# A one-column exponential behind each Gelu pass of a fused attention and MLP kernel

## The chip, the cores and the metric

The kernel runs on one core of one Trainium2 chip. The metric is the device time of one execution in microseconds; lower is better. The engines are called by short names in the profile: PE is TensorE (matmuls; PEld its weight loads), DVE is VectorE, ACT is ScalarE, POOL is GpSimd, SP is SyncE, which issues most of the DMAs.

## The reference

For one sequence of 2048 tokens of width 512 it computes two branches from the same input and mixes them by a gate of each token:

```python
g = _sigmoid((x * gate_w).sum(-1, keepdims=True))
a = _A_ref(x, A_wqkv, A_wo)              # attention, 32 heads of 16
b = _B_ref(x, B_w1, B_w2, B_w3, B_w4)
return g * a + (1 - g) * b

def _B_ref(x, w1, w2, w3, w4):
    h = _gelu(_layernorm(x, axis=-1) @ w1)
    ...   # four quarters of h shifted by 1, -1, 2, -2 tokens
    x1 = x + hs                          # hs: the shifted quarters @ w2
    h2 = _gelu(_layernorm(x1, axis=-1) @ w3) @ w4      # w3: 512 x 1792
    return x1 + h2
```

The Gelu is the tanh form. The attention is a full softmax: 32 heads times 2048 x 2048 scores.

## The kernel before, in words

The attention sets the length. Its scores are made in blocks of 128 keys by 512 queries. TensorE writes such blocks into the eight banks of PSUM (the product of q and kT, line 1320). Most blocks go to ScalarE, two at a time: one instruction takes the exponential of 128x1024 scores from the banks and writes it as bf16 into `prob` (line 1415). The other blocks go to VectorE, which makes an approximate exponential by working on the bits (line 1446) and adds shifts of it (line 1489); GpSimd makes a part of these shifts (line 1491). TensorE then multiplies the blocks of `prob` with V (line 1544). A slot of `prob` may be written again when the product that read it is done.

Between the attention's matmuls stand those of the MLP branch (helper `gen`, line 953): `w1`, then the first Gelu, then `w2`; later `w3`, the second Gelu, and `w4`. `hT` holds the first hidden layer, 128 x 4 x 2048. The second hidden layer, of width 1792, is worked on in chunks of 512 tokens, two chunks at a time (`PAIRS`), one in `hB` and one in the memory of `hT`. A Gelu is one ScalarE instruction over a whole layer or chunk, in place. So ScalarE makes three Gelu passes: one instruction of 128x8192 (`mlp1`, line 1187), and twice two instructions of 128x7168 (`mlp2`, line 1224). Everything else that ScalarE does is exponentials, besides a few copies at both ends.

The exponential and the Gelu need different function tables in ScalarE. The compiler puts a table load ahead of each activation whose function isn't in the table that is loaded: seven loads in all, one at the start, one ahead of each Gelu pass, and one ahead of the first exponential behind each pass. The program books a load to the line of the activation it belongs to. If an activation waits for several semaphores, the waits that don't fit on it stand ahead of it in the queue of its engine, and ahead of its table load.

The order of the instructions on each engine is set before the program runs. `Sim` is a model of the engines with costs written down in the kernel; `act(hold, deps, fn)` gives it a ScalarE job with an assumed duration and a function that emits the instruction. `Sim` plays the jobs through and writes down the order, and the functions are called in that order. The chip then runs each engine's instructions in that fixed order and holds an instruction back only until the data and buffers it needs are there. Small constant tiles that the change touches: `zero` (128x384, zeros, bf16) and `mb` (128x1, 32-bit), which at the start of the program helps to make the masks `mO` and `mE` and is not read later. At the start there is already one exponential of a column of `zero` (line 928), which brings the first table load.

Of the kernel before, what the change touches and what calls it, by code (L numbers as in the profile page):

```python
# [10 lines left out]
ACT = mybir.ActivationFunctionType  # L11
ALU = mybir.AluOpType
BF16 = mybir.dt.bfloat16
F32 = mybir.dt.float32
# [438 lines left out]
def kernel(  # L453
# [14 lines left out]
    nc = tc.nc  # L468
# [3 lines left out]
    S, D = x_flat.shape  # L472
    H, DH = 32, 16
    KT = D // P
# [3 lines left out]
    FT = F // P  # L478
# [268 lines left out]
    zero = const.tile([P, 384], BF16, name="zero")  # L747
# [8 lines left out]
    mb = const.tile([P, 1], mybir.dt.int32, name="mb")  # L756
# [8 lines left out]
    hT = const.tile([P, KT, S + 4], BF16, name="hT")  # L765
# [58 lines left out]
    def act(hold, deps, fn, **kw):  # L824
        return sim.add(Job("ACT", hold, 180.0, deps, fn, **kw))

    def gp(hold, deps, fn, **kw):
        return sim.add(Job("POOL", hold, 110.0, deps, fn, port=True, **kw))
# [15 lines left out]
    def W(name):  # L844
        return wb[name].slot
# [11 lines left out]
    def start(eng, lat, fn, hold=530.0):  # L857
# [11 lines left out]
                                                   in_=wrows(A_wqkv[:, n0:n1])))  # L869
# [15 lines left out]
    for k in range(KT):  # L885
# [5 lines left out]
                                                                        in_=x_src(c, 0, 4)))] for c in (2, 3)]  # L891
# [32 lines left out]
    for j in range(4):  # L924
        dma(2200.0, [j_wl], lambda j=j: nc.sync.dma_start(
            out=woL[32 * j + 1:32 * j + DH + 1, :], in_=A_wo[(25 + 2 * j) * DH:(26 + 2 * j) * DH, :]), prio=5)
# [19 lines left out]
    def gen(name, at, deps, mms, N=512, due=None):  # L946

        get = lambda: one(g.buf)
        units = []
        for i, mm in enumerate(mms):  # L950
            lf, rf = mm[:2]
            n0, n1, st, sp, ns = mm[2:] if len(mm) > 2 else (0, N, i == 0, i == len(mms) - 1, N * 0.42)
            units.append([Op("col", j, lambda j=j, lf=lf, rf=rf, n0=n0, n1=n1, st=st, sp=sp: nc.tensor.matmul(  # L953
                get()[32 * j:32 * j + 32, n0:n1], lhsT=lf(32 * j, 32 * j + 32), rhs=rf(), start=st, stop=sp,
                tile_position=(0, 32 * j), skip_group_check=True), ns=ns, name=name) for j in range(4)])
        if due is None:
            due = at + DUES[["w1", "w2", "w3", "w4"].index(name) if name in ("w1", "w2", "w3", "w4") else 0]
        g = Gen(units, deps, at, name, due=due)
        g.skew = True

        def by_rows(k, i):
            lf, rf = mms[k][:2]
            rows = slice(32 * i, 32 * i + 32)
            o = Op("row", i, lambda: nc.tensor.matmul(get(), lhsT=lf(0, P)[rows], rhs=rf()[rows], start=False, stop=True,  # L964
                                                      tile_position=(32 * i, 0), skip_group_check=True), name=name)
            o.dst = [g.buf]
            return o

        if name == "w4" and len(mms) > 5:
            g.by_rows = by_rows  # L970
        gens.append(g)
        return g

    def evac(g, hold, fn, prio=2, eng="DVE", **kw):
        job = Job(eng, hold, 165.0, [g.units[-1][-1]] if not COL else g.units[-1], lambda: fn(one(g.buf)), prio=prio,
                  frees=[g.buf] + kw.pop("frees", []), **kw)
        return sim.add(job)
# [148 lines left out]
    def stats(t, which, deps, at):  # L1126
        sb = Buf("st", 1)
        a = dve(600, deps, lambda: nc.vector.bn_stats(out=sb.slot[:], in_=x_sb[:, t, :]), prio=6, at=at, acq=[sb])  # L1128
        return dve(110, [a], lambda: nc.vector.bn_aggr(out=mv[which][:, t, :], in_=sb.slot[:]), prio=0, frees=[sb])
# [4 lines left out]
    def normalise(c, which, sj, at):  # L1134

        ts_ = slice(4 * c, 4 * c + 4)
        a = gp(150, sj, lambda: nc.gpsimd.tensor_scalar(out=rs[which][:, ts_], in0=mv[which][:, ts_, 1], scalar1=EPS,
                                                        scalar2=1.0, op0=ALU.add, op1=ALU.mult), prio=2)
        b = gp(1000, [a], lambda: nc.gpsimd.tensor_tensor(out=rs[which][:, ts_], in0=rs[which][:, ts_],
                                                          in1=mhalf[:, ts_], op=ALU.pow), prio=2)  # L1140
        m = dve(100, [b], lambda: nc.vector.scalar_tensor_tensor(
            out=nm[which][:, ts_], in0=mv[which][:, ts_, 0], scalar=-1.0, in1=rs[which][:, ts_], op0=ALU.mult,
            op1=ALU.mult), prio=1, port=True)
        ds = []
        last = []
        for t in range(4 * c, 4 * c + 4):
            xb = Buf("xn", 1)
            g = dve(323, [m], lambda t=t, xb=xb: nc.vector.tensor_scalar(  # L1148
                out=xb.slot[:], in0=x_sb[:, t, :], scalar1=rs[which][:, t:t + 1], scalar2=nm[which][:, t:t + 1],
                op0=ALU.mult, op1=ALU.add), prio=0.35, acq=[xb], port=True)  # L1150
            last.append(g)
            ds.append(dma(2600.0, [g], lambda t=t, xb=xb: nc.sync.dma_start(
                out=xn_dram[which, t * P:(t + 1) * P, :], in_=xb.slot[:]), frees=[xb]))
        tb = Buf("xnT", FT if which else KT)
        bx[which, c] = tb
        js = []
        for k in range(KT):
            js.append(dma(3600.0, ds, hold=1280.0, fn=lambda k=k: nc.sync.dma_start(
                out=tb.slot[:, k, :], in_=xn_dram[which, c * 512:(c + 1) * 512, k * P:(k + 1) * P], transpose=True),
                acq=[tb] if k == 0 else [], prio=4))  # L1160
            js[k].need = tb if k else None
        j_xnT[which, c] = js
        return last

    big1 = Buf("big", NT)

    def mlp1(at_of):
        sj = {}
        for t in range(NT):
            sj[t] = stats(t, 0, j_x[t // 4], at_of("s", t))  # L1170
        pre = []

        def alloc():
            nc.gpsimd.memset(hT[:, :, 0:2], 0.0)
            nc.gpsimd.memset(hT[:, :, S + 2:S + 4], 0.0)

        a0 = gp(250, [], alloc, prio=2, acq=[big1])
        for c in range(NCH):
            normalise(c, 0, [sj[t] for t in range(4 * c, 4 * c + 4)], 0)
            for m in range(KT):  # L1180
                g = gen("w1", at_of("w1", c * KT + m), j_xnT[0, c] + [dl_w["1"], a0],
                        [(lambda a, b, k=k, m=m: W("1")[:, k, m * P + a:m * P + b],
                          lambda k=k, c=c: bx[0, c].slot[:, k, :]) for k in range(KT)])
                g.ops[-1].frees += [bx[0, c], wb["1"]]
                pre.append(evac(g, PSUM_NS, lambda ps, c=c, m=m: nc.vector.tensor_copy(  # L1185
                    out=hT[:, m, 2 + c * 512:2 + (c + 1) * 512], in_=ps[:])))
        ge = act(93 + 1700 * KT + 3450, pre, lambda: nc.scalar.activation(
            out=hT[:, :, 2:2 + S], in_=hT[:, :, 2:2 + S], func=ACT.Gelu_apprx_tanh), prio=0)
        dshift = [1, -1, 2, -2]
        s2 = {}  # L1190
        for t in range(NT):
            g = gen("w2", at_of("w2", t), [ge, dl_w["2"]],
                    [(lambda a, b, j=j, t=t: hT[:, j, 2 + t * P - dshift[j] + a:2 + t * P - dshift[j] + b],
                      lambda j=j: W("2")[:, j, :]) for j in range(KT)])
            g.ops[-1].frees += [big1, wb["2"]]
            e = evac(g, PSUM_NS, lambda ps, t=t: nc.vector.tensor_tensor(out=x_sb[:, t, :], in0=x_sb[:, t, :],
                                                                          in1=ps[:], op=ALU.add))
            s2[t] = stats(t, 1, [e], 0)
        return s2
# [20 lines left out]
    def mlp2(cs, s2, at_of, jgate):  # L1220
        ups = [mlp2_up(c, s2, at_of, jgate) for c in cs]
        pre = [j for u in ups for j in u[0]]
        for n, (c, (_, bb, h2, jx1g)) in enumerate(zip(cs, ups)):
            ge = act(93 + 427 * FT + (0 if n else 2750), pre, lambda h2=h2: nc.scalar.activation(
                out=h2(), in_=h2(), func=ACT.Gelu_apprx_tanh), prio=-1)
            mlp2_down(c, ge, bb, h2, jx1g, at_of)

    def mlp2_down(c, ge, bb, h2, jx1g, at_of):
# [406 lines left out]
    for r0, (c, G) in enumerate((c, G) for c in range(NCH) for G in range(4)):  # L1635
# [6 lines left out]
        if r0:  # L1642
            q_proj(G, c, 128 * r0 - QAT)
    s2 = mlp1(at_of)
    gate_job = jg[0]
    for i in range(KT):
# [7 lines left out]
    for cs in PAIRS:  # L1654
        mlp2(cs, s2, at_of, gate_job)
# [318 lines left out]
```

## Time and profile before

| | |
|---|---|
| Median of 3 runs | 754.83 us (753.9 to 755.6) |
| The profiled execution's own time | 750.92 us |
| Its span, from first to last instruction | 749.1 us |
| Granted TensorE clock | 1.000 |
| Exponentials of 128x1024 on ScalarE | 750, 688.7 us busy |
| Gelu instructions on ScalarE | one of 7.04 us, four of about 6.17 us |
| Table loads on ScalarE | seven, 1283 ns each |

Times in the views are microseconds from the start of the span. A row of the view by time gives start, length, engine, line, operation, output and inputs, and in brackets the idle time of the engine before it with what ended that. A row of the list of waits gives who waited for whom: total, number of times, longest. A row of the groups gives count, busy time and mean duration in ns of one, and behind the next bar the idle time before them.

### The profile page before, as it was taken

The page shows a single profiled execution, that of the slowest core. Times are in us where ns is not written, and L with a number is a line of the kernel's source. Part 1 is how long each engine was busy: PE and PEld are TensorE (multiplying, and loading weights), DVE is VectorE, ACT ScalarE, POOL GpSimd, SP SyncE. Part 2 cuts the span into 40 slices and gives each one's busy share as a digit, 9 for nine tenths or more (in the row PEclk, how much of TensorE's full clock was granted, in tenths as well). Part 3 has the DMA queues.
Part 4 walks back from the last instruction along what each step waited for, and adds up shares of the span by engine and source line. Part 5 has one row for each costly group of instructions (what it writes and reads, how often), then busy time and mean ns, then how long its engine had stood idle before and what let it go on. Part 6 is the DMA issues. An engine that isn't in the chain of part 4 may idle for free.

```text
span 749.1 us, 23684 instructions
## 1 busy us (share of the span) xinstructions
PE 735.9 (98%) x9516; PEld 211.6 (28%) x9516; DVE 689.9 (92%) x1450; ACT 733.0 (98%) x771; POOL 423.3 (57%) x422
## 2 busy tenths in 40 slices
PE   8999999999999999999999999999999999999997
PEld 5343222232222222222322222222222232222222
DVE  5899999998999999999899999998999889989987
ACT  7999999999999999999999999999999999999996
POOL 2355667687674665566555432646767645553552
PEclk9999999999999999999999999999999999999999
DMA  9413322012122211034000110011100000101001
GB/s 197 146 34 85 83 62 49 19 47 79 54 65 68 63 28 49 20 81 109 10 25 9 38 36 27 14 28 47 25 20 21 21 12 28 27 25 21 7 21 47
DMA packets 67095, 34.60 MB, mean 46 GB/s; under 512 B 46749, under 2 KB 62381, under 8 KB 66985
## 3 DMA queue, kind: packets, MB, share of 16 engines
q1 hardware_dynamic: 66040, 32.56, 17.4%
q8 instruction: 74, 1.21, 0.7%
q10 hardware_dynamic: 944, 0.52, 0.2%
q14 instruction: 37, 0.29, 0.1%
HBM read 17.40 MB, written 6.81 MB: 32 GB/s over the span
## 4 chain that ended last, share of the span: by engine, by line
PE 86%; ACT 7%; DVE 4%; issue 2%; POOL 0%; DMA 0%; ACTq 0%; DVEq 0%; POOLq 0%
PE banks L1544 30%; PE banks L1320 30%; PE banks L953 25%; ACT prob L1415 6%; DVE prob L1446 1%; DVE prob L1489 1%; PE banks L932 0%; POOL prob L1491 0%; ACT L1415 0%; DVE st L1128 0%; DVE kT L1025 0%; DMA xn_dram<-xn 0%; PE banks L984 0%; DVE hT L1185 0%; DVE xn L1148 0%
## 5 line engine op out<-in xcount | busy, mean ns | idle before, releaser
L1415 ACT ACTIVATE prob<-banks 128x1024 bf16<-128x1024 f32 x750 | 688.7, 1149 | 1.1 <-PE banks L1320 0.6
L1491 POOL TENSOR_SCALAR prob<-prob 128x1024 uint16<-128x1024 uint16 x360 | 370.2, 1045 | 280.5 <-DVE prob L1489 145.5
L1446 DVE TENSOR_SCALAR prob<-banks 128x512 uint16<-128x512 f32 x549 | 364.1, 684 | 30.3 <-PE banks L1320 25.0
L1544 PE MATMUL banks<-prob,V 128*17 128x512 bf16 (+1 forms) x3695 | 321.3, 382 | 1.2 <-POOL prob L1491 0.7
L1320 PE MATMUL banks<-q,kT 32*128 32x512 bf16 x2048 | 282.7, 385 | 6.1 <-ACT prob L1415 3.4
L1489 DVE TENSOR_SCALAR prob<-prob 128x1024 uint16<-128x1024 uint16 (+1 forms) x465 | 181.2, 434 | 5.3 <-PE banks L1544 2.5
L1320 PEld LDWEIGHTS <-kT 32*128 32x128 bf16 x2048 | 71.1, 91 | 316.4 <-ACT prob L1415 291.0
L1544 PEld LDWEIGHTS <-V 128*17 128x17 bf16 (+1 forms) x3695 | 72.0, 88 | 117.3 <-issue 97.8
L953 PE MATMUL banks<-xnT,w 128*32 128x512 bf16 x1152 | 98.0, 383 | 0.0
L953 PE MATMUL banks<-w,hT 128*32 128x512 bf16 x688 | 63.8, 384 | 0.0
L1583 POOL TENSOR_TENSOR oT<-accsb,bcs 128x512 bf16<-128x512 f32 x31 | 39.8, 1282 | 28.5 <-DVE prob L1489 14.4
L953 PEld LDWEIGHTS <-w 128*32 128x32 bf16 x1936 | 42.4, 95 | 47.3 <-issue 27.7
L953 PE MATMUL banks<-w,w 128*32 128x256 bf16 (+1 forms) x784 | 39.1, 308 | 0.1
L953 PE MATMUL banks<-w,hB 128*32 128x512 bf16 x448 | 37.3, 382 | 0.0
L964 PE MATMUL banks<-wo,oD 32*128 32x512 bf16 x76 | 28.8, 385 | 0.0
L1565 DVE COPY accsb<-banks 128x512 f32<-128x512 f32 x31 | 21.2, 685 | 1.4 <-PE banks L1544 1.0
L1128 DVE BATCH_NORM_STATS2 st<-x_sb 128x6 f32<-128x512 bf16 x32 | 21.8, 685 | 0.0
L953 PE MATMUL banks<-w,wq 128*32 128x512 bf16 x256 | 20.9, 383 | 0.0
L953 PEld LDWEIGHTS <-hT 128*32 128x32 bf16 x688 | 14.8, 95 | 19.1 <-issue 14.9
L953 PE MATMUL banks<-wo,oD 128*32 128x512 bf16 x164 | 20.0, 385 | 0.1
L1217 DVE CAST hB<-banks 128x512 bf16<-128x512 f32 x28 | 19.0, 680 | 1.1 <-PE banks L953 1.1
L1217 DVE CAST hT<-banks 128x512 bf16<-128x512 f32 x28 | 19.0, 680 | 0.4 <-PE banks L953 0.4
(95 smaller groups left out, 262.1 us busy)
## 6 DMA issues: line engine op xcount, KB each, us to landing
bcs<-rr SPq DMA_DIRECT2D x124, 64.0 KB, 2.1
xn_dram<-xn SPq DMA_DIRECT2D x32, 128.0 KB, 1.8
w<-in_B_w_dram SPq DMA_DIRECT2D x5, 512.0 KB, 7.8
oD<-oT SPq DMA_DIRECT2D x124, 16.0 KB, 2.1
w<-in_B_w_dram SPq DMA_DIRECT2D x4, 448.0 KB, 3.2
out_dram<-ot SPq DMA_DIRECT2D x14, 128.0 KB
x_sb<-in_A_x_dram SPq DMA_DIRECT2D x3, 512.0 KB
w<-in_A_wqkv_dram SPq DMA_DIRECT2D x2, 256.0 KB, 5.8
```

The lines of the kernel that those rows point to most:

```text
L953: units.append([Op("col", j, lambda j=j, lf=lf, rf=rf, n0=n0, n1=n1, st=st, sp=sp: nc.tensor.matmul(get()[32 * j:32 * j + 32, n0:n1], lhsT ...
L964: o = Op("row", i, lambda: nc.tensor.matmul(get(), lhsT=lf(0, P)[rows], rhs=rf()[rows], start=False, stop=True, tile_position=(32 * i, 0), ...
L1128: a = dve(600, deps, lambda: nc.vector.bn_stats(out=sb.slot[:], in_=x_sb[:, t, :]), prio=6, at=at, acq=[sb])
L1217: pre.append(evac(g, PSUM_NS, lambda ps, m=m: nc.vector.tensor_copy(out=h2()[:, m, :], in_=ps[:])))
L1320: o = Op("row", i, lambda: nc.tensor.matmul(dst(), lhsT=kT[G][32 * i:32 * i + 32, kt * P:(kt + 1) * P], rhs=qbuf[G, c].slot[32 * i:32 * i ...
L1415: job = act(hold, ops, lambda: nc.scalar.activation(out=prob[:, pb.cut(), :].bitcast(BF16), in_=unit()[:, rb.cut(), :], func=ACT.Exp, scal ...
L1446: return nc.vector.tensor_scalar(out=prob[:, b0.cut() if w == 2 else b0.bufs[h0].slot, :], in0=unit()[:, rb.cut() if w == 2 else rb.bufs[0 ...
L1489: return nc.vector.tensor_scalar(out=cut(k), in0=cut(0), scalar1=float(SHIFT * k), scalar2=None, op0=ALU.add)
L1491: return nc.gpsimd.tensor_scalar(out=cut(k), in0=cut(0 if both else 2), scalar1=1.0, scalar2=float(SHIFT * (k if both else 1)), op0=ALU.mu ...
L1544: return nc.tensor.matmul(one(accs[r])[32 * i:32 * i + n, :], lhsT=lhs(n), rhs=rhs(), start=st and not edge, stop=True, tile_position=(0, ...
L1565: e = dve(PSUM_NS, round_ops[r], lambda: nc.vector.tensor_copy(out=ab.slot[:], in_=one(accs[r])), acq=[ab], prio=0, frees=[accs[r], Call(a ...
L1583: n = gp(1250, d3, lambda: nc.gpsimd.tensor_tensor(out=ob.slot[:], in0=ab.slot[:], in1=bb.slot[:], op=ALU.mult), acq=[ob], frees=[ab, bb], ...
```

## The change

A helper `gelu` emits the Gelu instruction and, where `back` is set, an exponential of one column of zeros behind it, written into `mb`. `back` is set for the pass of `mlp1` and for the second of the two instructions of each pair in `mlp2`, so there are three such exponentials. The assumed durations given to `Sim` are the same as before.

```diff
+    def gelu(ap, back):
+        g = nc.scalar.activation(out=ap, in_=ap, func=ACT.Gelu_apprx_tanh)
+        if back:
+            nc.scalar.activation(out=mb[:].bitcast(F32), in_=zero[:, 0:1], func=ACT.Exp)
+        return g
+
     def mlp1(at_of):
...
-        ge = act(93 + 1700 * KT + 3450, pre, lambda: nc.scalar.activation(
-            out=hT[:, :, 2:2 + S], in_=hT[:, :, 2:2 + S], func=ACT.Gelu_apprx_tanh), prio=0)
+        ge = act(93 + 1700 * KT + 3450, pre, lambda: gelu(hT[:, :, 2:2 + S], True), prio=0)
...
         for n, (c, (_, bb, h2, jx1g)) in enumerate(zip(cs, ups)):
-            ge = act(93 + 427 * FT + (0 if n else 2750), pre, lambda h2=h2: nc.scalar.activation(
-                out=h2(), in_=h2(), func=ACT.Gelu_apprx_tanh), prio=-1)
+            ge = act(93 + 427 * FT + (0 if n else 2750), pre,
+                     lambda h2=h2, back=n == len(cs) - 1: gelu(h2(), back), prio=-1)
             mlp2_down(c, ge, bb, h2, jx1g, at_of)
```

## The prediction

> **What bounds the kernel now.** I read the page first: span, engine shares, the chain that ended last.
>
> ```profile
> span 749.1 us, 23684 instructions
> PE 735.9 (98%) x9516; PEld 211.6 (28%) x9516; DVE 689.9 (92%) x1450; ACT 733.0 (98%) x771; POOL 423.3 (57%) x422
> PE 86%; ACT 7%; DVE 4%; issue 2%; POOL 0%; DMA 0%; ACTq 0%; DVEq 0%; POOLq 0%
> ```
>
> TensorE and ScalarE both stand at 98%, and the chain hardly touches anything else: DMA and GpSimd have 0% of it. So a saving counts only if it moves ScalarE and TensorE together. Next I asked which waits those two have, from the costliest groups and the list of waits.
>
> ```profile
> L1415 ACT ACTIVATE prob<-banks 128x1024 bf16<-128x1024 f32 x750 | 688.7, 1149 | 1.1 <-PE banks L1320 0.6
> ...
> ACT L1415 <- PE banks L1544: 2.8, 3, 1.4
> PE banks L1320 <- ACT prob L1415: 3.4, 5, 1.1
> ```
>
> The 750 softmax exponentials wait 1.1 us in all, so ScalarE runs through them nearly without a gap. The second row is the table load that the program books to the exponential's line: three of them, idle for 2.8 us together, released by TensorE's prob x V products. The third is TensorE's visible wait for exponentials: 3.4 us in five places. So I looked at ScalarE's order of time around the three Gelu passes, since they make those loads necessary.
>
> ```profile
> 160.83 1.28 ACT L1187 ACT_TABLE_LOAD   x1
> 162.12 7.04 ACT L1187 ACTIVATE hT<-hT 128x8192 bf16<-128x8192 bf16 x1
> 170.54 1.28 ACT L1415 ACT_TABLE_LOAD   x1 [1.38 <-PE banks L1544]
> 171.83 11.11 ACT L1415 ACTIVATE prob<-banks 128x1024 bf16<-128x1024 f32 x12
> ...
> 347.11 1.28 ACT L1224 ACT_TABLE_LOAD   x1
> 348.40 6.18 ACT L1224 ACTIVATE hB<-hB 128x7168 bf16<-128x7168 bf16 x1
> 354.48 6.16 ACT L1224 ACTIVATE hT<-hT 128x7168 bf16<-128x7168 bf16 x1
> 361.48 1.28 ACT L1415 ACT_TABLE_LOAD   x1 [0.83 <-PE banks L1544]
> 362.77 3.77 ACT L1415 ACTIVATE prob<-banks 128x1024 bf16<-128x1024 f32 x4
> ...
> 602.88 6.16 ACT L1224 ACTIVATE hT<-hT 128x7168 bf16<-128x7168 bf16 x1
> 609.60 1.28 ACT L1415 ACT_TABLE_LOAD   x1 [0.56 <-PE banks L1544]
> 610.89 3.77 ACT L1415 ACTIVATE prob<-banks 128x1024 bf16<-128x1024 f32 x4
> ```
>
> Each time the pass ends, ScalarE sits idle for 1.38, 0.83 or 0.56 us, loads the table for 1.28 us, and only then starts the exponential. The idle time and the load stand one behind the other although the load needs nothing that TensorE makes. The chain shows why: the wait of the first exponential stands ahead of the load in ScalarE's queue.
>
> ```profile
> 361.43 0.02 ACTq L1415
> 361.48 1.28 ACT L1415
> ...
> 609.55 0.02 ACTq L1415
> 609.60 1.28 ACT L1415
> ```
>
> The queue's wait (ACTq, start and length) ends at 361.45 and 609.57, and the load begins 0.03 us later. In the built order of the kernel before, the wait on TensorE's semaphore stands in front of the load at all three places.
>
> **The change part by part.** Built, the changed kernel has the same instructions with the same waits in the same order on TensorE, VectorE, GpSimd and SyncE. On ScalarE there are three more activations of 128x1. The number of table loads stays at seven: the load behind each Gelu now belongs to the small exponential, which waits for nothing, and the wait on TensorE stands behind both, at the first real exponential. No DMA is moved, and mb, which is written, was last read at the start of the program.
>
> *The loads.* The passes end at 162.12 + 7.04 = 169.16, 354.48 + 6.16 = 360.64 and 602.88 + 6.16 = 609.04. If the load follows at once, it is over 1.28 later: 170.44, 361.92, 610.32. Does a load follow at once? Behind an exponential it does: the Gelu loads at 160.83 and 347.11 show no idle time before them. Behind a Gelu no row shows it, as all three stand behind a wait; the third bounds a tail of the pass to 0.56 us. I take nothing, as the rows behind exponentials are the nearest, and price the 0.56 as a rival.
>
> The Trainium skill ("ScalarE: Activation LUTs", section "What ACT_TABLE_LOAD costs") says that every switch costs about 1283 ns of load plus about 1380 ns of drain. The load agrees with the 1.28 of the rows; the drain is not a fixed part here, for the third load stood 0.56 us behind its Gelu and the load at 347.11 had no idle time before it. By that sum nothing could be gained at any of the three places.
>
> *The small exponential.* One like it stands at the start of the program.
>
> ```profile
> L928 ACT ACTIVATE zc<-zero 128x1 f32<-128x1 bf16 x1 | 0.2, 202 | 0.0
> ```
>
> It took 0.20 us from start to end. Neighbouring activations overlap: the first 7168-wide pass ends at 348.40 + 6.18 = 354.58 and the second begins at 354.48, so 0.10 of the 0.20 lies beside the next one. It costs between 0.10 (overlapped) and 0.20 (not), in the path all three times; it cannot cost less than nothing, as nothing else shrinks for it. With 0.01 between load and activation the real exponentials can start at 170.55, 362.03 and 610.43, or 0.10 later each.
>
> *The wait of TensorE's products* does not vanish: it now runs beside the load. It ended just before 170.54, 361.48 and 609.60, at the latest; the first of these is all but level with the new start, the others lie 0.55 and 0.83 earlier. The real exponential also waits for a GpSimd operation. Counting GpSimd's increments up to the awaited value, these are:
>
> ```profile
> 168.97 1.04 POOL L1491 TENSOR_SCALAR prob<-prob 128x1024 uint16<-128x1024 uint16 x1 [0.76 <-DVE prob L1489]
> ...
> 359.03 1.04 POOL L1491 TENSOR_SCALAR prob<-prob 128x1024 uint16<-128x1024 uint16 x1 [1.78 <-DVE prob L1489]
> 603.95 1.04 POOL L1491 TENSOR_SCALAR prob<-prob 128x1024 uint16<-128x1024 uint16 x1 [0.79 <-DVE prob L1489]
> ```
>
> They end at 170.01, 360.07 and 604.99, ahead of the new starts. So the exponentials come earlier by 171.83 - 170.55 = 1.28, 362.77 - 362.03 = 0.74 and 610.89 - 610.43 = 0.46: 2.48 us, or 2.18 without the overlap.
>
> *What TensorE makes of it.* Its waits at these three places:
>
> ```profile
> 172.91 0.40 PE L1320 MATMUL banks<-q,kT 32*128 32x512 bf16 x4 [1.15 <-ACT prob L1415]
> ...
> 363.85 0.39 PE L1320 MATMUL banks<-q,kT 32*128 32x512 bf16 x1 [1.05 <-ACT prob L1415]
> 611.97 0.39 PE L1320 MATMUL banks<-q,kT 32*128 32x512 bf16 x4 [0.74 <-ACT prob L1415]
> ```
>
> These three are 1.15 + 1.05 + 0.74 = 2.94 of its 3.4 us. At the first place its own work lasts until 172.91 - 1.15 = 171.76, so it gains 1.15 at most; at the others the exponential sets the gain. TensorE's gain: 1.15 + 0.74 + 0.46 = 2.35, or 1.15 + 0.64 + 0.36 = 2.15. What is late next would be VectorE, were it busy there; it isn't:
>
> ```profile
> 174.93 0.69 DVE L1196 TENSOR_TENSOR x_sb<-x_sb,banks 128x512 bf16<-128x512 bf16 x1 [1.20 <-PE banks L953]
> ...
> 365.90 0.43 DVE L1489 TENSOR_SCALAR prob<-prob 128x1024 uint16<-128x1024 uint16 x1 [1.07 <-PE banks L1544]
> 612.44 1.29 DVE L1446 TENSOR_SCALAR prob<-banks 128x512 uint16<-128x512 f32 x2 [0.90 <-PE banks L1320]
> ```
>
> It idles 1.20, 1.07 and 0.90 behind TensorE, each at least what is gained there. So all three busy engines move earlier together, and behind that ScalarE runs without gaps, which hands the shift on. I take 2.2 us, near the lower sum, for small losses on the way. Against the profiled execution: 750.92 us (span 749.1 and 1.8 around it) less 2.2 is 748.7, with a span of 746.9. The median of the runs, 754.83, lies 3.9 above that execution; the saving does not depend on that, so I subtract it there: **752.6 us**, 0.29% less. What a measurement of this kernel can tell from no change is about 0.2%, 1.5 us; the saving is only half as much again.
>
> **The rivals.** *The pass has a tail.* The engine finishes a Gelu before it can change tables, so that the load cannot follow at once. By the third row the tail is at most 0.56. Then the loads end at 171.00, 362.48 and 610.88, the exponentials start 0.11 later, and the gains are 0.72, 0.18 and -0.10: 0.8 us, 754.0. For it: no row shows a load straight behind a Gelu. Against it: the loads behind exponentials. Chance 0.12. The drain of the Trainium skill (same page and section) is this mechanism at about 1.38; the third row excludes that size, not a smaller one.
>
> *The gain is given back.* The schedule fixes every engine's order, and the next passes wait for chains through VectorE, GpSimd and DMA. If such a chain, not ScalarE, sets the start of a later stage, what was won before it is lost there. Losing all of the first gain leaves 2.35 - 1.15 = 1.2, 753.6. For it: VectorE's 92%. Against: DMA has 0% of the chain, and VectorE's work is released by the engines that move. Chance 0.12.
>
> *Slower: VectorE and GpSimd meet differently.* VectorE's shifts of a probability block vary with what runs beside them:
>
> ```profile
> L1489 DVE TENSOR_SCALAR prob<-prob x465: 293/421/1380, 12.0 to 739.7; 128x1024 uint16<-128x1024 uint16 x154, 128x512 uint16<-128x512 uint16 x1
> ```
>
> Work that starts about 1 us earlier from 171 on puts them beside other GpSimd operations. A median one of 0.42 that takes twice as long, well within the row's ends, costs 0.42. From six of them on, all in the path, the gain is gone (2.2 / 0.42 = 5.2); nine more than now make it slower by 9 x 0.42 - 2.2 = 1.6 us, 756.4. Against it: as many should get shorter, and VectorE has 4% of the chain. Chance 0.05.
>
> *It does nothing.* The exponential comes at the same time after all, for instance because the products it waits for come later when ScalarE is earlier: 754.8. Against it: up to the end of the first pass nothing is changed, so there the products come when they came. Chance 0.04.
>
> **How the numbers follow.** Forecast 0.67, tail 0.12, given back 0.12, slower 0.05, nothing 0.04. The forecast's own range is 752.2 to 753.2: the sums of 2.5 down to 2.15 and half a microsecond for the spread of medians. The range of 8 in 10 reaches up to the tail's 754.0 and its spread, and down as far as all of TensorE's 2.94 plus the same spread: **751.2 to 754.4**. Faster by over 0.2%: the forecast with nearly all of its chance and a little of the given-back case, 0.68. Slower: 0.06. The rest, 0.26, is within 0.2%.
>
> **What would show it.** Right: each load behind a Gelu with no idle time before it, at 169.2, 360.6 and 609.0 less what earlier places won; the small exponential 0.2 long; the first real one 0.1 to 0.2 after its start; TensorE's wait for exponentials down from 3.4 to about 1 us or less. Wrong: a load that starts some tenths after the Gelu (tail); a real exponential still waiting on L1544 (nothing); all three gaps gone but the third pass less than 1.5 us earlier (given back); more busy time in L1489 (slower).

## The result, and the profile after

Over 12 runs each the changed kernel takes 750.38 us (median, 749.16 to 752.74) and the kernel before 753.78 us (751.18 to 755.6); the ratio is 0.9959, 95% interval 0.9946 to 0.9973. So it is faster by 0.41%, 3.4 us between these medians. The forecast was 752.6 with a range of 751.2 to 754.4: the direction held, the time lies 0.8 us below the range. All the runs of both kernels in this study, taken together, give means of 753.44 (123 runs) and 750.74 (36 runs), a difference of 2.70 us with a 95% interval of about 2.2 to 3.2 (from spreads of 1.54 and 1.31 us between runs). The runs were made on several chips; the means of the kernel before on three of them are 753.44, 753.36 and 753.63. Two disturbed executions, one of 1204.63 us (the profiled one of the experiment with four more exponentials, whose profile is therefore not read) and one of 1520.57 us (the kernel before with more buffers), are left out of every number below.

What follows is from the page of the profile after; its execution took 749.34 us. Lines of the kernel that follow the edit are numbered 5 higher than before: 1420 is the exponential (1415 before), 1325 q x kT, 1549 prob x V; 1168 is the Gelu and 1170 the small exponential.

```profile
span 747.5 us, 23687 instructions
PE 735.4 (98%) x9516; PEld 211.2 (28%) x9516; DVE 688.8 (92%) x1450; ACT 733.3 (98%) x774; POOL 422.9 (57%) x422
PE 81%; ACT 11%; DVE 4%; issue 1%; DMA 1%; POOL 0%; SPq 0%; ACTq 0%; DVEq 0%; POOLq 0%
```

The three busy engines have the same shares as before, and the chain that ended last still runs through TensorE and ScalarE (81% and 11%, before 86% and 7%). ScalarE's order of time around the three passes:

```profile
161.66 1.28 ACT L1168 ACT_TABLE_LOAD   x1
162.96 7.04 ACT L1168 ACTIVATE hT<-hT 128x8192 bf16<-128x8192 bf16 x1
170.01 1.28 ACT L1170 ACT_TABLE_LOAD   x1
171.30 0.20 ACT L1170 ACTIVATE mb<-zero 128x1 f32<-128x1 bf16 x1
171.41 11.09 ACT L1420 ACTIVATE prob<-banks 128x1024 bf16<-128x1024 f32 x12
...
360.21 1.28 ACT L1170 ACT_TABLE_LOAD   x1
361.50 0.20 ACT L1170 ACTIVATE mb<-zero 128x1 f32<-128x1 bf16 x1
361.61 4.66 ACT L1420 ACTIVATE prob<-banks 128x1024 bf16<-128x1024 f32 x5
...
607.93 1.28 ACT L1170 ACT_TABLE_LOAD   x1
609.22 0.20 ACT L1170 ACTIVATE mb<-zero 128x1 f32<-128x1 bf16 x1
609.33 5.58 ACT L1420 ACTIVATE prob<-banks 128x1024 bf16<-128x1024 f32 x6
```

The idle times are gone. The first load stands 0.01 us behind the end of its Gelu (162.96 + 7.04 = 170.00), the small exponential takes 0.20, and the real one starts 0.11 behind its start. From the groups and the list of waits:

```profile
L1170 ACT ACT_TABLE_LOAD x3 | 3.8, 1283 | 0.0
L1170 ACT ACTIVATE mb<-zero 128x1 f32<-128x1 bf16 x3 | 0.6, 203 | 0.0
...
PE banks L1325 <- ACT prob L1420: 1.0, 4, 0.3
```

The loads wait 0.0 us where they waited 2.8, and TensorE's visible wait for exponentials fell from 3.4 to 1.0 us. One row goes the other way: the exponentials wait 2.1 us in all, where they waited 1.1.

```profile
L1420 ACT ACTIVATE prob<-banks 128x1024 bf16<-128x1024 f32 x750 | 688.7, 1150 | 2.1 <-PE banks L1325 1.7
...
77.44 11.11 ACT L1420 ACTIVATE prob<-banks 128x1024 bf16<-128x1024 f32 x12 [0.83 <-PE banks L1325]
88.91 1.95 ACT L1420 ACTIVATE prob<-banks 128x1024 bf16<-128x1024 f32 x2 [0.37 <-PE banks L1325]
```

The two waits that make this up stand at 77 and 89 us, ahead of the first pass and so ahead of everything that the change touches. TensorE and VectorE at the places where they idled before:

```profile
172.53 0.40 PE L1325 MATMUL banks<-q,kT 32*128 32x512 bf16 x4
...
362.67 0.38 PE L1325 MATMUL banks<-q,kT 32*128 32x512 bf16 x1 [0.31 <-ACT prob L1420]
610.39 0.40 PE L1325 MATMUL banks<-q,kT 32*128 32x512 bf16 x4 [0.29 <-ACT prob L1420]
...
174.49 0.69 DVE L1201 TENSOR_TENSOR x_sb<-x_sb,banks 128x512 bf16<-128x512 bf16 x1
364.72 0.43 DVE L1494 TENSOR_SCALAR prob<-prob 128x1024 uint16<-128x1024 uint16 x1 [0.41 <-PE banks L1549]
610.85 1.29 DVE L1451 TENSOR_SCALAR prob<-banks 128x512 uint16<-128x512 f32 x2 [0.45 <-PE banks L1325]
```

TensorE's waits were 1.15, 1.05 and 0.74 and are none, 0.31 and 0.29; VectorE's 1.20, 1.07 and 0.90 are none, 0.41 and 0.45. Counted from the end of the first Gelu, TensorE's matmul comes after 172.53 - 170.00 = 2.53 us, before after 172.91 - 169.16 = 3.75.

The trace, cut at ScalarE's table loads and first exponentials, shows where the time came from. All rows are worked out from starts and ends of ScalarE's instructions, in microseconds:

| Stretch | before | before, 2nd | before, 3rd | after | after, 2nd | after, 3rd |
|---|---|---|---|---|---|---|
| start to first exponential | 8.87 | 9.25 | 8.74 | 8.63 | 8.63 | 9.16 |
| from there to the load of pass 1 | 151.96 | 153.89 | 155.11 | 153.03 | 152.56 | 153.47 |
| end of pass 1 to next exponential | 2.68 | 2.68 | 2.69 | 1.42 | 1.42 | 1.42 |
| from there to the load of pass 2 | 175.27 | 176.24 | 175.27 | 175.25 | 175.46 | 175.91 |
| end of pass 2 to next exponential | 2.13 | 2.13 | 2.13 | 1.41 | 1.41 | 1.41 |
| from there to the load of pass 3 | 232.73 | 232.73 | 232.73 | 232.76 | 232.67 | 232.67 |
| end of pass 3 to next exponential | 1.85 | 1.84 | 1.84 | 1.41 | 1.41 | 1.41 |
| from there to ScalarE's last | 134.90 | 134.92 | 134.89 | 134.87 | 134.89 | 134.86 |

The three short stretches differ by kernel and by nothing else: 1.26 + 0.72 + 0.44 = 2.42 us. The long ones behind pass 2 and 3 agree within 0.1 us, so nothing of the saving is lost there. The first long stretch, which no edit touches, varies by 3 us between profiles of one and the same program, and the one between pass 1 and 2 by 1 us.

### The profile page after: what moved, and what is told of

Same layout as the page of the kernel before. It is cut to its first block, busy times and chain, and to the rows that moved or that the text cites. A ratio compares the mean times of both kernels' runs of the same rounds, so it can differ in the third digit from the quotient of the medians.

```text
span 747.5 us, 23687 instructions
## 1 busy us (share of the span) xinstructions
PE 735.4 (98%) x9516; PEld 211.2 (28%) x9516; DVE 688.8 (92%) x1450; ACT 733.3 (98%) x774; POOL 422.9 (57%) x422
## 4 chain that ended last, share of the span: by engine, by line
PE 81%; ACT 11%; DVE 4%; issue 1%; DMA 1%; POOL 0%; SPq 0%; ACTq 0%; DVEq 0%; POOLq 0%
PE banks L1549 29%; PE banks L1325 29%; PE banks L953 23%; ACT prob L1420 7%; ACT hB L1168 2%; ACT hT L1168 2%; DVE prob L1451 1%; DVE prob L1494 1%; PE banks L932 0%; ACT L1168 0%; DVE hT L1191 0%; DVE accsb L1570 0%; DMA den<-accsb 0%; DMA xn_dram<-xn 0%; DMA pk<-den 0%
```

## The experiments

Three theories were at stake. Theory 1: the change saves 2.4 us, all behind the three passes, and the rest of the 3.4 us between the medians is spread of the runs. Theory 2: about a microsecond more is saved where the profiles don't show it. Theory 3, formed after the first four: the spread lies at a few places where an engine waits for a DMA to land, and hits both kernels alike.

### Both kernels again

No edit.

> The kernel before, timed against itself: it shows how far two sets of runs of one program stand apart. Theory 1 (the change saves 2.4 us, all of it behind the three Gelu passes: 1.27 + 0.72 + 0.44; what the medians show beyond that is spread of the runs): this pair differs by up to about 1 us although nothing differs, and in the profile the stretch from the first exponential to the first Gelu's table load, which was 151.96 us before and 153.03 with the change, comes out at some third value within about a microsecond of these. Theory 2 (the change saves some 3.4 us, a microsecond of it where the profiles do not show it): this pair agrees within 0.3 us.

> The changed kernel again, in the same company as the three others. Theory 1: 2.4 us faster than before, give or take 0.7; the real exponential starts 1.41 us after each Gelu pass, as in the first profile of the change. Theory 2: 3.4 us faster, and the stretches from first exponential to first table load are shorter than before in both profiles.

The kernel before against itself: median 752.68, ratio 0.9992 (0.9973 to 1.0011), beside a median of 753.45 in 35 runs that reach from 750.95 to 757.92. The change again: 750.13, ratio 0.9959 (0.994 to 0.9978). Equal programs stand 0.8 us apart in their medians, so theory 2's condition (0.3 us) failed; in their means they stand 0.28 apart, so this is a weak sign. The change shows 0.9959 a second time: 3.3 us between the medians, more than theory 1 allows (2.4 give or take 0.7), and 2.9 between the means, which it allows. Theory 2's other sign doesn't show: the stretch up to the first Gelu's load was to be shorter with the change, and its 153.03 and 152.56 us lie between the 151.96 and 153.89 of the kernel before. Matching the two profiles of the kernel before, exponential by exponential, the second one falls behind in steps near 72, 88 and 250 us. VectorE near 85 us, first the kernel before, then the same again:

```profile
84.77 0.88 DVE L1148 TENSOR_SCALAR xn<-x_sb,rs,nm 128x512 bf16<-128x512 bf16 x2 [0.62 <-DMA xn_dram<-xn]
```

```profile
86.49 0.41 DVE L1148 TENSOR_SCALAR xn<-x_sb,rs,nm 128x512 bf16<-128x512 bf16 x1 [1.12 <-DMA xn_dram<-xn]
87.57 0.41 DVE L1148 TENSOR_SCALAR xn<-x_sb,rs,nm 128x512 bf16<-128x512 bf16 x1 [0.66 <-DMA xn_dram<-xn]
```

VectorE can't write the next normalised block until the write of an earlier one out of the same buffer has landed, 0.62 us in one run, 1.12 and 0.66 in the other. The step near 250 us comes with GpSimd's wait for a broadcast; waits and ScalarE's order of time in the second profile of the kernel before:

```profile
POOL oT L1583 <- DMA bcs<-rr: 1.6, 1, 1.6
...
252.88 3.89 ACT L1415 ACTIVATE prob<-banks 128x1024 bf16<-128x1024 f32 x4 [0.71 <-PE banks L1320]
```

### One part of the change alone

```diff
-                     lambda h2=h2, back=n == len(cs) - 1: gelu(h2(), back), prio=-1)
+                     lambda h2=h2, back=False: gelu(h2(), back), prio=-1)
```

> The small exponential stands behind the first Gelu pass alone. Theory 1: the time from Gelu end to real exponential is 1.41, 2.13 and 1.85 us at the three places (2.68 at the first before), and the kernel is 1.27 us faster than before. Theory 2: more than 2 us faster. Rival (the first place's gain is lost further on, since TensorE or VectorE sets the start of the second pass): under 0.6 us faster, with the stretch from the first real exponential behind pass one to the table load of pass two longer than 175.3 us.

```diff
-        ge = act(93 + 1700 * KT + 3450, pre, lambda: gelu(hT[:, :, 2:2 + S], True), prio=0)
+        ge = act(93 + 1700 * KT + 3450, pre, lambda: gelu(hT[:, :, 2:2 + S], False), prio=0)
```

> The small exponential stands behind the second and third pass, not behind the first. Theory 1: 2.68, 1.41 and 1.41 us from Gelu end to real exponential, and 0.72 + 0.44 = 1.16 us faster than before; together with the kernel that has it at the first place alone, the two savings add up to that of the whole change. Theory 2: about 2 us faster. Rival (gains are lost further on): under 0.5 us.

The first alone: 752.28, ratio 0.9994 (0.9974 to 1.0013). The last two alone: 752.72, 0.9997 (0.9979 to 1.0014). Both intervals hold theory 1's saving (0.9983 and 0.9985) and also none; as times they are inconclusive, and theory 2's 2 us lie just outside of the first and clearly outside of the second. The means save 0.86 and 0.33 us. Together that is 1.2, against 2.70 for the whole change: 1.5 short, with an uncertainty of 1.3 (95%). The expectation that the two savings add up did not come true in the times, and the runs don't say why. The profiles are clear. First place alone, then the last two alone; the rows are those of places without a small exponential:

```profile
363.52 1.28 ACT L1420 ACT_TABLE_LOAD   x1 [0.83 <-PE banks L1549]
```

```profile
172.71 1.28 ACT L1420 ACT_TABLE_LOAD   x1 [1.38 <-PE banks L1549]
```

The old waits of 0.83 and 1.38 are back exactly where the small exponential is missing; from Gelu to exponential it is 1.42, 2.13, 1.85 in the one and 2.68, 1.41, 1.41 in the other, as expected. The rival of a lost first gain needed more than 175.3 us from there to pass 2: it was 176.37 with the first alone, but the kernel before has 176.24 in one of its own profiles and the whole change 175.25 in one. Both long stretches have the same visible reason: GpSimd waits for its broadcast, 1.76 us near 247 with the first alone and 1.61 near 248 in that profile of the kernel before.

### The small instruction without the load

```diff
-            nc.scalar.activation(out=mb[:].bitcast(F32), in_=zero[:, 0:1], func=ACT.Exp)
+            nc.scalar.activation(out=mb[:].bitcast(F32), in_=zero[:, 0:1], func=ACT.Gelu_apprx_tanh)
```

> The small activation behind each pass is a Gelu of the same column instead of an exponential: the added instruction is there, but it needs no other table, so the load stays at the first real exponential and behind its wait. Theory 1 (only the load's place matters): 2.68, 2.13 and 1.85 us from Gelu end to real exponential as before, since the 0.2 us of the small one lie in the time that ScalarE waits anyway; the same time as before within what the runs can tell (0.9985 to 1.0015). Rival (a further instruction behind the pass helps by itself, or shifts the program's code to a better place): about 1 us or more faster than before.

752.77, ratio 0.9988 (0.9974 to 1.0002): no change that can be told. ScalarE around the first pass:

```profile
170.83 0.19 ACT L1170 ACTIVATE mb<-zero 128x1 f32<-128x1 bf16 x1
172.31 1.28 ACT L1420 ACT_TABLE_LOAD   x1 [1.29 <-PE banks L1549]
173.60 2.85 ACT L1420 ACTIVATE prob<-banks 128x1024 bf16<-128x1024 f32 x3
```

The small instruction is there and the wait is still ahead of the load. From Gelu to exponential it is 2.68, 2.12 and 1.85. The saving is that of the load's place.

### Delays of known length

```diff
             nc.scalar.activation(out=mb[:].bitcast(F32), in_=zero[:, 0:1], func=ACT.Exp)
+            for _ in range(12):                      # 4 and 8 in the two others
+                nc.scalar.activation(out=gwz[:].rearrange("p k c -> p (k c)"), in_=zero[:, 0:128], func=ACT.Exp)
```

> The whole change, and twelve exponentials of 128 columns into a tile that is no longer needed behind each small one. One should take 0.3 us (0.2 of the small one and 128 x 0.8 ns), so that the real exponentials start some 12 x 0.3 = 3.6 us later at each of the three places; the profile tells the delay. Theory 1 (ScalarE sets the pace, so what is lost or won behind a pass is lost or won in the whole): the time rises over that of the change by the sum of the three delays, about 11 us, with a slope of 0.9 to 1.0, and the stretches between the passes keep their length. Rival (TensorE's and VectorE's work hides or gives back a part): a slope under 0.7, with shorter stretches after a longer delay.

> The whole change with four exponentials of 128 columns behind each small one, a delay too short to leave TensorE without work for long. Twelve of them delayed each place by 3.95 us and cost more than they took: in that profile TensorE's clock was granted at half for 6.8, 3.4 and 3.4 us behind the three places. Theory 1 (what ScalarE loses or wins behind a pass is lost or won in the whole, one for one, as long as the clock stays up): each place 1.3 us later, 3.9 us in all, and the time 3.5 to 4.5 us over that of the change, with the clock at 1.00 behind all three places and the stretches between them as long as before. Rival (the slope is above one without the clock): 5.5 us or more over the change.

> Eight more exponentials behind each small one, between the two doses. Each place 2.6 us later, 7.9 us in all. If a gap in TensorE's work of some 2.5 to 3 us lets the clock fall, the time is 10 to 13 us over that of the change and the page of the clock shows it at half behind some of the places; if not, 7.5 to 8.5 us over it.

| Added behind each pass | delay at the three places, from the profile | time (mean) over that of the change |
|---|---|---|
| 4 | none read; 3 x 1.3 = 3.9 as an estimate from the others | 4.5 (± 1.3) |
| 8 | 2.59 + 2.58 + 2.59 = 7.8 | 12.2 (± 1.8) |
| 12 | 3.95 + 3.95 + 3.95 = 11.9 | 17.5 (± 1.0) |

Means are over 11, 6 and 6 runs, against 750.74. With four the cost is one for one within its spread, as theory 1 has it. That the clock stays up there is not shown: five of the eleven runs have a granted clock of 0.993 to 0.997 and take 755.2 to 758.4 us. The six with 0.999 or more have a mean of 753.66, 3.4 us over that of the change's 22 runs with such a clock (750.24). With twelve theory 1's slope of 0.9 to 1.0 failed, upwards: 17.5 / 11.9 = 1.5. The cause is in the windows of that profile (PE busy, PEld, DVE, ACT, POOL, granted clock, DMA), behind the first and second pass:

```profile
176.00:182.70 6.70, 6.00 (x46) 1.34 (x46) 2.67 (x6) 4.99 (x6) 2.53 (x3) 0.50 0.24 69
...
374.00:377.40 3.40, 3.40 (x30) 0.60 (x26) 0.43 (x1) 2.32 (x3) 0.04 (x1) 0.52 0.00 0
```

TensorE ran at half its clock for 6.8 us behind the first pass and 3.4 behind each of the others. The stretches that follow the three passes are 177.92, 234.04 and 136.25 us long, 2.7, 1.3 and 1.4 more than with the change. With the delays that makes 11.9 + 5.4 = 17.3 of the 17.5 us. With eight, where the 12.2 us lie in the 10 to 13 that were expected if the clock falls, TensorE's waits at the three places and the windows:

```profile
175.68 0.40 PE L1327 MATMUL banks<-q,kT 32*128 32x512 bf16 x4 [2.46 <-ACT prob L1422]
...
368.46 0.58 PE L1327 MATMUL banks<-q,kT 32*128 32x512 bf16 x1 [2.90 <-ACT prob L1422]
620.30 0.40 PE L1327 MATMUL banks<-q,kT 32*128 32x512 bf16 x4 [2.88 <-ACT prob L1422]
...
176.00:182.70 6.70, 6.70 (x93) 1.83 (x90) 4.97 (x11) 6.70 (x8) 5.15 (x5) 1.00 0.23 71
...
368.50:371.90 3.40, 3.40 (x28) 0.59 (x29) 0.00 (x0) 2.59 (x3) 0.00 (x0) 0.50 0.00 0
...
621.10:624.50 3.40, 3.40 (x31) 0.46 (x23) 2.86 (x8) 2.68 (x4) 0.09 (x1) 0.50 0.02 5
```

The gap of 2.46 left the clock up, those of 2.90 and 2.88 did not. The stretches behind them show the price: 175.24 us behind the first pass, as without the delay, and 234.30 and 136.25 behind the others, 1.6 and 1.4 more. The gaps of the kernel before at these three places, 1.15 at most, had no such cost in any of its three profiles.

### Both kernels a third time

No edit.

> The kernel before once more, for a third profile. Theory 3 (what the runs differ by lies at a few places where VectorE or GpSimd wait for a DMA to land, and hits both kernels alike): the stretch up to the first Gelu's load falls between 160.8 and 163.2 us after the start, as in the profiles so far, by how long VectorE waits for the write of the normalised tokens near 85 us; behind pass one all stretches keep within 0.3 us of those of the other profiles but the one near 249 us, where GpSimd can wait for its broadcast. Rival (the changed program's DMAs land earlier in every run): over 162 us here, and always under 162 us for the change.

> The changed kernel once more, for a third profile, and to put the runs of all sets together. Theory 1 and 3: 1.41 us from Gelu end to real exponential at all three places; the median saves 2.4 us, give or take 0.7; the stretch to the first load can be any of those seen with the kernel before. Rival (the changed program's DMAs land earlier): under 162 us to the first load for the third time, and 3 us or more saved.

The kernel before: 752.85, ratio 1.0002 (0.9982 to 1.0022). The change: 750.70, ratio 0.9967 (0.995 to 0.9985), 2.5 us less than the 753.19 of the kernel before in the same set, as theory 1 has it. The rival fell: the change's load of pass 1 came at 9.16 + 153.47 = 162.6 us, over 162. Theory 3's range held for the change and not for the kernel before, whose load came at 163.85, later than the 163.2 given. There VectorE's wait near 85 us was 2.15 us, the longest in the three profiles of the kernel before, and the clock fell on top of it; windows of the third profile of the kernel before:

```profile
86.70:90.10 3.40, 1.89 (x24) 0.59 (x21) 3.40 (x9) 1.78 (x3) 1.29 (x2) 1.00 0.23 77
90.10:93.50 3.40, 3.40 (x24) 0.69 (x21) 3.29 (x7) 2.38 (x3) 1.81 (x2) 0.51 0.20 46
```

### Without the wait near 85 us

```diff
+            xt = lambda t=t, xb=xb: xb.slot[:] if which else hB[:, t % FT * 512:(t % FT + 1) * 512]
-                out=xb.slot[:], in0=x_sb[:, t, :], scalar1=rs[which][:, t:t + 1], scalar2=nm[which][:, t:t + 1],
+                out=xt(), in0=x_sb[:, t, :], scalar1=rs[which][:, t:t + 1], scalar2=nm[which][:, t:t + 1],
...
-                out=xn_dram[which, t * P:(t + 1) * P, :], in_=xb.slot[:]), frees=[xb]))
+                out=xn_dram[which, t * P:(t + 1) * P, :], in_=xt()), frees=[xb]))
```

> The change, and the normalised tokens of the first MLP layer are written to a part of hB of their own for each block of 128 tokens instead of two buffers in turn; every engine's order stays. VectorE then need not wait near 85 us until the write of an earlier block to memory has landed. Theory 3 (that landing is what the runs differ by, besides the broadcast near 249 us): the wait of the line that makes xn on a DMA is gone from the profile (1.0 to 2.7 us in the profiles so far), the first Gelu's load comes under 162 us, and the runs are 1 to 2 us faster than those of the change, with less spread. Rival (the wait is replaced by the one for the transposed reads that follow): no faster.

> The same buffers for the kernel before, without the small exponentials. Theory 1: with the change it is 2.4 us less (1.27 + 0.72 + 0.44), and as both now start with less spread, the difference of the two stands out clearer: 1.9 to 2.9. Theory 2 (a microsecond of the change's saving lies elsewhere): 3.4 us or more between the two. Theory 3: 1 to 2 us faster than the kernel before.

With the change: 748.27 (6 runs), ratio to the kernel before 0.9932 (0.9907 to 0.9957). Without it: 751.09 (11 runs), 0.997 (0.9953 to 0.9987). Each is 2.1 us faster in its mean than the same kernel with two buffers (748.66 against 750.74, 751.33 against 753.44), with uncertainties of about 1.1 and 0.7. VectorE at that place, without the change:

```profile
85.19 0.73 DVE L1149 TENSOR_SCALAR hB<-x_sb,rs,nm 128x512 bf16<-128x512 bf16 x2
```

No wait; the line waits for a DMA nowhere in these two profiles. The mean difference between the pair is 2.68 us, nearest to theory 1; with its uncertainty of 0.6 (one standard error) it excludes neither 2.4 nor 3.4. The spread between runs became smaller without the change (1.54 to 1.06 us) and hardly with it (1.31 to 1.25, over six runs only). One expectation failed: the profile with the change has its first load at 163.6 us. There VectorE waited 2.6 us for another landing, that of the sums of a round of attention (pk<-den) near 71 us, and the clock was at half from 73.8 to 77.2; that run took 751.13, the slowest of the six. The version with both edits is the fastest of this study.

## Why the prediction was right or wrong

**The loads: right.** They follow the Gelu at once, 0.01 us behind it. The tail rival (up to 0.56) is excluded by the change itself. The Trainium skill ("ScalarE: Activation LUTs", section "What ACT_TABLE_LOAD costs") gives about 1380 ns of drain for each switch beside the load; the change's three loads behind a Gelu stand without any idle time, so no such part exists here, and what looked like it (1.38 at the first place) was the wait for TensorE.

**The small exponential: right.** 0.20 us long, 0.11 of it in the path.

**The exponentials' gain: right.** 1.28 + 0.74 + 0.46 = 2.48 foreseen, 1.26 + 0.72 + 0.44 = 2.42 shown.

**TensorE's share: a little low.** The step "it gains 1.15 at most" at the first place and the "small losses on the way" took the sum from 2.48 to 2.2. Neither shows: TensorE's matmul at the first place comes 3.75 - 2.53 = 1.22 us earlier, the stretch from the first exponential to pass 2 is 175.25 us against 175.27, so ScalarE's full 1.26 went through, and nothing was lost behind pass 2 and 3. The sum was too low by 0.2 us.

**The step that failed: the base and its spread.** The prediction subtracted from 754.83, the median of three runs, and gave "half a microsecond for the spread of medians". All 123 runs of the kernel before reach from 750.95 to 758.53 with a standard deviation of 1.5 us, and their mean is 753.44, 1.4 below the base. The profile had hinted at it: the profiled execution, 3.9 us under the median, was taken to be a matter apart. (The ranges also don't come out of their own terms: 754.83 - 2.5 - 0.5 is 751.8 and not 752.2, 754.83 - 2.94 - 0.5 is 751.4 and not 751.2; the measured time lies below all of these.) Of the 2.2 us between 752.6 and 750.38, 1.05 are the base (754.83 to the 753.78 of the 12 runs compared), and 0.2 the sum (2.2 to 2.42). The other 1.0 is the difference between 2.42 and the 3.4 of those medians; over all runs it is 0.3 (2.70 against 2.42), which the interval of 2.2 to 3.2 allows to be nothing.

Much of the spread goes with the clock that TensorE was granted. Of the 111 runs of the kernel before that have it on record, the 76 with 0.999 or more have a mean of 752.75, the 12 with 0.995 or less one of 756.76. Among runs with 0.999 or more the two kernels differ by 752.75 - 750.24 = 2.50 us (76 and 22 runs, 95% interval 2.1 to 2.9); with any lower bound from 0.997 to 1.000 it is 2.5 to 2.6, and never over 3.0 at the upper end. That agrees with the 2.42 of the profiles and leaves no room for theory 2's 3.4. Whether some 0.5 us more is saved where the profiles don't show it stays open, and so does the shortfall of the two parts.

**The rivals.** Given back: no, see the stretches. VectorE and GpSimd meeting differently: line 1494 (1489 before) has a mean of 430 ns against 434, no loss. Nothing happens: no.

## What to carry to other kernels

A table load stands behind the waits of the activation that it is made for; where ScalarE comes out of one function into a wait, a tiny activation of the next function that waits for nothing puts the load beside the wait, for 0.11 us. At the three places it was worth the old wait less 0.11 or 0.12 us (1.38, 0.83 and 0.56 became 1.26, 0.72 and 0.44), and all of that counted because TensorE and VectorE idled there too. The first of these waits is already longer than the load (1.28); much longer ones were not tried, and as only the load is moved, no more than its length can be won. Before a forecast of a few tenths of a per cent, look at how far single runs of one kernel differ, and take the base and the range from that and not from a median of three.

## What had not been expected of the hardware

A gap in TensorE's work has a price beyond its length. Where TensorE was without work for 2.9 us, or busy for only 1.89 of 3.4 us, its clock was granted at half for the next 3.4 us; behind gaps of about 4 us (3.81, 4.26 and 4.25) it was so for 6.8, 3.4 and 3.4. That made a delay of 11.9 us cost 17.5. The half-clock stretches do not start at any moment: with twelve they start at 175.89, 373.86 and 626.45 us, which is 58 and 74 times 3.413 us apart, with eight at 368.52 and 621.11, again 74 times. The Trainium skill ("TensorE: Matmul & The Clock Gate", Part 1) describes a free-running window of 3413 ns; these starts and the lengths of 3.41 and 6.83 us agree with it. Its table puts the fall "after ≥1 idle window (~3.4µs)", and there the runs differ: in the 3.4 us ahead of a fall TensorE was busy for anything from 0 to 1.9 us. The runs give no threshold either, for in one such stretch with 1.69 us of work (the profile with eight, 173.96 to 177.37) the clock stayed up.

Waits for a DMA differ from run to run: VectorE's near 85 us was one of 0.62 us in one profile and one of 2.23 in another (the first place alone). Taking this wait away made both kernels about 2 us faster, but a spread of 1.1 to 1.3 us between runs stayed, so it is a part of the spread and not the whole.
